# Attention and a gated MLP on one core: GpSimd makes and stores the later score bounds, weight parts go out two in ten score products, output steps pause at product ends and group changes

## The chip, the cores and the metric

The kernel runs on one core of a Trainium2 chip. The metric is the device time of one execution in microseconds (us). The engines are TensorE (PE in the profile; PEld is its loading of weights), VectorE (DVE), ScalarE (ACT), GpSimd (POOL) and SyncE (SP, which here only issues DMAs). Each engine works through its own instructions in order; waits on other engines are semaphores.

## The reference

A transformer block with pre-normalisation, 2048 rows of width 512, all in float32: attention with 32 query heads of 16 elements that share one key and one value head, then a gated MLP of width 1792.

```python
def _A_ref(x, wq, wk, wv, wo):
    B, S, D = x.shape
    H = 32
    Dh = D // H
    q = (lambda x, *d: x.transpose(*d))((x @ wq).reshape(B, S, H, Dh), 0, 2, 1, 3)
    k = x @ wk
    v = x @ wv
    scores = jnp.einsum("bhqd,bkd->bhqk", q, k) * (Dh ** -0.5)
    p = _softmax(scores, axis=-1)
    o = jnp.einsum("bhqk,bkd->bhqd", p, v)
    return (lambda x, *d: x.transpose(*d))(o, 0, 2, 1, 3).reshape(B, S, H * Dh) @ wo

def _B_ref(x, w_gate, w_up, w_down):
    return (_gelu(x @ w_gate) * (x @ w_up)) @ w_down

h = x + _A_ref(_layernorm(x, axis=-1), A_wq, A_wk, A_wv, A_wo)
h2 = h + _B_ref(_layernorm(h, axis=-1), B_w_gate, B_w_up, B_w_down)
```

## The kernel before

**Tiling.** The 2048 rows of queries are four blocks b of 512. The 32 heads are eight groups g of four. For each block and group the keys run in 16 chunks kc of 128. One score step, `score(n)`, makes two heads' scores of one key chunk (two matmuls into a tile s, 128 x 1024) and lets ScalarE take the exponential into p (L410). Two steps, n and n+1, are a pair; 32 steps are a group, 256 a block. TensorE weighs the values with p two pairs later (`weigh`, L414, accumulator acc), and after a group's last chunk `evacuate` copies acc to oT on VectorE (L427).

**Numbers in two parts.** Matmul operands are split into a high part and the rest (hi and lo), so one product is three matmuls. Queries are kept in DRAM (q_d) with a row per head for a bound on the scores, which stands in for the softmax's maximum; `load_q` (L386) brings a group's queries back as qg, two pairs after the group before it has begun.

**Block 0's stage.** Beside the scores of block 0 three things run. First, the projections of the later blocks' queries (`project_q`): a chunk's product is done in two halves of TensorE's rows, two matmuls at a time beside the scores. After the first half VectorE copies one column of the bank (mark, L210), and TensorE's second half waits for it. After the second half VectorE copies the bank out (pq_raw, L225), splits it (qh, ql), and squares it (qs). There is one bank, so the next product waits for the copy. Once a block's four chunks are done, a small matmul sums the squares per head (pqn, L259), VectorE copies it (qn, one buffer) and takes its maximum into q2, GpSimd works out two factors from it in four small instructions (`factors`, L269 to L278), and VectorE makes the bound's row m from qn and the factors (`bound`, L285), which SP stores to q_d (L289). The list `after` holds factors and bound with a count of pairs; `age` runs down the counts and places the step in the program when its count is out: factors after 2, the bound after 4.

Second, the split of the MLP's and wo's weights into parts (`part_weights`, 46 parts): SP loads 256 KB into w_raw (L514), AHEAD_W parts ahead, GpSimd casts the high part (L119) and subtracts (L120) into w_both (two buffers), and stores 512 KB to DRAM from its own queue (L523, L529). One part goes out each time the loop calls `next(parts)`: every second pair in which `after` is empty (L1109).

Third, the outputs of the groups. `evacuate` stores oT to DRAM (L431); `turn_out` (L440) reads it back with the layout turned, as oc; then VectorE inverts the sums (L454, four reciprocals), multiplies (divide, L457), and makes o_hi (L465) and o_lo (L469). In block 0 these steps wait in the list `outs`, one entry taken at the end of each pair (`take_out`), with eight empty entries between the reading back and the reciprocals.

**Order.** In this stage the order of SP, VectorE, TensorE, GpSimd and ScalarE is the order in which the program is written; nothing reorders it. At n = 256 what is left of parts and bounds is put out, and the dense work of block 0 (wo, then the MLP) begins; its tiles take the place of w_raw, w_both and the rest.

Of the kernel before, what the change touches and what calls it, by code (L numbers as in the profile page):

```python
# [9 lines left out]
F32 = mybir.dt.float32  # L10
# [9 lines left out]
P = 128  # L20
# [9 lines left out]

W2 = 3

AHEAD_W = 3

LAST_Q = 240

# [16 lines left out]
def kernel(  # L53
# [12 lines left out]
    nc = tc.nc  # L66
    x = x.flatten_outer_dims()
    out = out.flatten_outer_dims()
    S, D = x.shape
    DH = wk.shape[1]  # L70
# [9 lines left out]
    KC = S // P  # L80
# [27 lines left out]
    q_d = dram.tile([H, KR, S], F32R, name="q_d")  # L108
# [49 lines left out]
    def run(outer, first):  # L158
# [10 lines left out]
        def psum1(name):  # L169
            return ps.tile([P, T], F32, tag="d", bufs=width, name=name)  # L170
# [16 lines left out]
        def project_q(b, cs, eng, col, whole=None):  # L187
            halves = whole is not None
            whole = whole if halves else cs
            tsl = slice(b * T, (b + 1) * T)  # L190
            xT_hi, xT_lo = xT[b]
            urgent = b == 0 and cs[0] == 0
            qss = []
            for c in cs:
                pq = psum1(f"pq_{b}_{c}")
                terms = [
                    (wt[:, d, c * P : (c + 1) * P], xt[:, d, :])
                    for d in range(DC)
                    for wt, xt in ((wq_hi, xT_hi), (wq_hi, xT_lo), (wq_lo, xT_hi))
                ]  # L200
                last = len(terms) - 1
                full = c in whole
                for n, (lhsT, rhs) in enumerate(terms if full else ()):
                    nc.tensor.matmul(pq, lhsT, rhs, start=(n == 0), stop=(n == last))  # L204
                    if n % 3 == 2 and (urgent or n < last):
                        yield 3
                for a in range(2) if not full else ():
                    if a:
                        mark = eb.tile([P, 1], F32, tag="qmark", bufs=2, name=f"mark_{b}_{c}")
                        nc.vector.tensor_copy(mark, pq[:, :1])  # L210
                    rows = slice(64 * a, 64 * a + 64)
                    for n, (lhsT, rhs) in enumerate(terms):
                        yield a, last - n, partial(
                            nc.tensor.matmul, pq, lhsT[rows], rhs[rows],
                            start=(a == 0 and n == 0), stop=(a == 1 and n == last),
                            skip_group_check=True,
                        )

                raw = None
                if (b, c) in HURRY or not full:  # L220
                    raw = eb.tile([P, T], F32, tag="vT", bufs=3, name=f"pq_raw_{b}_{c}")
                    if b == 0:
                        nc.scalar.activation(raw, pq, AF.Copy)
                    else:
                        nc.vector.tensor_copy(raw, pq)  # L225
                    if full:
                        yield 3
                if halves and norms:
                    yield REST
                    norms.pop()()  # L230
                qh = eb.tile([P, T], F32R, tag="qh", bufs=2, name=f"qh_{b}_{c}")
                ql = eb.tile([P, T], F32R, tag="ql", bufs=2, name=f"ql_{b}_{c}")
                if raw is not None:
                    split(nc.vector, qh, ql, raw)
                else:

                    split(nc.vector if b == 0 and c == FIRST_Q else eng, qh, ql, pq)
                qs = eb.tile([P, T], BF16, tag="qs", bufs=DC, name=f"qs_{b}_{c}")
                square = partial(
                    (nc.gpsimd if urgent else nc.vector).tensor_tensor,  # L240
                    qs, qh.bitcast(F32), qh.bitcast(F32), op=ALU.mult,
                )
                if full:
                    square()
                else:
                    squares.append(square)
                qss.append(qs)
                for r0, part in ((0, qh), (DH, ql), (2 * DH, qh)):
                    nc.sync.dma_start(
                        q_d[c * HC : (c + 1) * HC, r0 : r0 + DH, tsl].bitcast(F32),  # L250
                        part.bitcast(F32),
                    )
                if not halves and (raw is None or b == 0):
                    yield 3

            def norm():
                pn = psum1(f"pqn_{b}_{cs[0]}")[:H, :]
                for i, c in enumerate(cs):
                    nc.tensor.matmul(  # L259
                        pn, sel[:, c, :], qss[i], start=(i == 0), stop=(i == len(cs) - 1)  # L260
                    )
                qn = eb.tile([H, T], F32, tag="qn", bufs=1, name=f"qn_{b}_{cs[0]}")
                nc.vector.tensor_copy(qn, pn)
                nc.vector.tensor_reduce(q2[:, col : col + 1], qn, axis=AX.X, op=ALU.max)

                mm = eb.tile([H, 3], F32, tag="mm", bufs=2, name=f"mm_{b}_{cs[0]}")

                def factors():
                    nc.gpsimd.tensor_scalar(  # L269
                        mm[:, 0:1], q2[:, col : col + 1], k2m, 1e-30, op0=ALU.mult, op1=ALU.add  # L270
                    )
                    nc.gpsimd.tensor_tensor(
                        mm[:, 1:2], mm[:, 0:1], power[:H, 0:1], op=ALU.pow
                    )
                    nc.gpsimd.tensor_scalar(
                        mm[:, 2:3], mm[:, 0:1], mm[:, 1:2], 0.5, op0=ALU.mult, op1=ALU.mult
                    )
                    nc.gpsimd.tensor_scalar(  # L278
                        mm[:, 1:2], mm[:, 1:2], k2m, 0.5, op0=ALU.mult, op1=ALU.mult
                    )  # L280

                m = eb.tile([H, T], F32R, tag="m", bufs=2, name=f"m_{b}_{cs[0]}")

                def bound():
                    nc.vector.tensor_scalar(  # L285
                        m, qn, mm[:, 1:2], mm[:, 2:3], op0=ALU.mult, op1=ALU.add
                    )
                    hs = slice(cs[0] * HC, (cs[-1] + 1) * HC)
                    nc.sync.dma_start(q_d[hs, 3 * DH, tsl].bitcast(F32), m[hs].bitcast(F32))  # L289

                if not urgent:
                    after.extend([[2, factors], [4, bound]])
                return qn, mm, m, factors

            if halves:
                norms.append(norm)
                return
            qn, mm, m, factors = norm()
            if urgent:
                yield 2  # L300
                factors()
                nc.scalar.activation(
                    m, qn, AF.Identity, bias=mm[:, 2:3], scale=mm[:, 1:2]
                )
                ms[b] = m
            else:
                yield 2


        after, squares, norms = [], [], []  # L310
        ms = {}
        q_first = project_q(0, range(FIRST_Q), nc.scalar, 0)
        q_rest = project_q(0, range(FIRST_Q, DC), nc.scalar, NB)
# [78 lines left out]
        o_blk, pair, outs, last_out = {}, [None], [], []  # L392
# [32 lines left out]
        def evacuate(b, g, acc):  # L425
# [61 lines left out]
            if last:  # L487
                last_out.extend([piece, gather])
            elif k == 1:

                if b == 0:
                    outs.extend([[] for _ in range(8)])
                    outs.extend([partial(invert, t)] for t in range(TB))
                    outs.extend([step] for step in (divide, high, low))
                else:
                    outs.append([])
                    outs.extend([partial(invert, t), partial(invert, t + 1)] for t in (0, 2))
                    outs.append([divide, high, low])
# [7 lines left out]
        def part_weights(pw):  # L506
# [3 lines left out]


            def load_f(src, name):
                raw = pw.tile([P, D], F32, tag="w_raw", bufs=AHEAD_W + 1, name=f"{name}r")
                nc.sync.dma_start(raw.rearrange("p (c n) -> p c n", n=src.shape[-1]), src)  # L514
                return raw

# [21 lines left out]
            for f in range(FC):  # L538
                fs = slice(f * P, (f + 1) * P)
                for k, src in enumerate((wg_t, wu_t)):  # L540
                    name = f"w1{f}_{k}"
# [4 lines left out]
                name = f"w2{f}"  # L546
# [505 lines left out]
        n, lead = 0, 2 * PER + sum(SIZES[: LEAD[0]])  # L1052
        with tc.manual_schedule(engines={mybir.EngineType.SP, mybir.EngineType.DVE}):
            parts, said = None, 3 if first else 0
            if first:
                work = later_q()
                parts = part_weights(early.enter_context(tc.tile_pool(name="parts", bufs=1)))
# [13 lines left out]
            while n < lead:  # L1071
# [6 lines left out]
                if n == 2 * PER:  # L1078
# [7 lines left out]
                    parts = work = None  # L1086
# [17 lines left out]
                    finish(1)  # L1104
                while squares:
                    squares.pop(0)()
                if outs:
                    take_out()
                if parts is not None and n % 4 == 0 and not after:  # L1109
                    next(parts, None)  # L1110
            assert n == lead
        assert not outs
# [421 lines left out]
```

## Time and profile before

| what | us |
|---|---|
| three runs, median | 1423.63 |
| three runs, lowest and highest | 1416.68, 1423.84 |
| the profiled execution | 1423.06 |
| its span, first to last instruction | 1421.1 |
| TensorE busy | 1400.7 (99%) |
| ScalarE busy | 1044.7 (74%) |
| VectorE busy | 549.0 (39%) |
| GpSimd busy | 180.1 (13%) |

The span goes from the first to the last instruction; the execution's time has what lies around it too. A share of busy time is a mean over stages. In the rows that follow, a line begins with its start in us and its length, or with its place in the code (L410); "out<-in" are the tiles that an instruction writes and reads, buffer numbers left out; in square brackets stands how long the engine was idle before and what ended that. The rows of a window give its length, then the busy time and instructions of each engine.

### The profile page before, as it was taken

How to read it: one execution, taken by the hardware profiler on the slowest of the kernel's cores; microseconds unless marked ns; L12 is line 12 of the kernel's file. 1: busy time of each engine (PE TensorE's matmuls, PEld its weight loads, DVE VectorE, ACT ScalarE, POOL GpSimd, SP SyncE). 2: the span in 40 equal slices, each digit the busy share in tenths (PEclk: the TensorE clock that was granted, in tenths of full speed). 3: DMA queues.
4: the chain of work that ended last, by engine and by line, in shares of the span. 5: the costliest groups of instructions: out<-in, count | busy, mean ns of one | idle time of the engine just before them, and what ended most of it. 6: DMA issues, size and time to landing. Idle time of an engine off the chain costs nothing.

```text
span 1421.1 us, 25578 instructions
## 1 busy us (share of the span) xinstructions
PE 1400.7 (99%) x10622; PEld 776.6 (55%) x10622; DVE 549.0 (39%) x984; ACT 1044.7 (74%) x1149; POOL 180.1 (13%) x272
## 2 busy tenths in 40 slices
PE   9999999999999999999999999999999999999998
PEld 7533333334555555555555555555565555557886
DVE  7413221314352332514252332413343342427665
ACT  7699998997787787777777777877788777772000
POOL 6365466400000000000000000000000000002000
PEclk9999999999999999999999999999999999999999
DMA  4477777733242242214252332223243241435551
GB/s 158 160 237 270 216 255 256 239 122 119 86 146 94 87 145 82 91 47 165 95 166 80 99 134 85 88 82 123 94 139 116 86 146 37 143 122 196 183 200 61
DMA packets 84699, 193.68 MB, mean 136 GB/s; under 512 B 9676, under 2 KB 24012, under 8 KB 84544
## 3 DMA queue, kind: packets, MB, share of 16 engines
q1 hardware_dynamic: 77208, 165.65, 35.4%
q0 software_dynamic: 7200, 26.22, 5.0%
q8 instruction: 85, 1.39, 0.4%
q14 instruction: 38, 0.31, 0.1%
q10 hardware_dynamic: 168, 0.10, 0.0%
HBM read 142.12 MB, written 49.55 MB: 135 GB/s over the span
## 4 chain that ended last, share of the span: by engine, by line
PE 87%; DMA 4%; ACT 3%; POOL 2%; DVE 1%; issue 1%; SPq 1%; DVEq 0%; POOLq 0%; ACTq 0%
PE acc L414 30%; PE s L406 18%; PE pu L928 9%; PE pg L928 8%; PE pd L928 5%; PE pd L605 3%; PE pd L627 3%; ACT p L410 3%; PE pg L627 3%; PE pu L627 3%; PE pp L605 2%; PE pq L404 2%; PE pq L204 1%; DMA w_0r<-in_B_w_gate_dram 1%; DMA w_d<-w_1b 1%
## 5 line engine op out<-in xcount | busy, mean ns | idle before, releaser
L410 ACT ACTIVATE p<-s 128x1024 f32<-128x1024 f32 x1024 | 973.3, 1029 | 233.9 <-PE s L406 232.0
L414 PE MATMUL acc<-p,v_sb 128*32 128x512 f32 x4096 | 499.4, 600 | 1.1 <-DVE oT L427 1.1
L406 PE MATMUL s<-qg,kaug 50*128 50x512 f32 x1984 | 419.4, 427 | 3.6 <-ACT p L410 3.6
L406 PEld LDWEIGHTS s<-qg,kaug 50*128 50x128 f32 x1984 | 191.5, 184 | 256.6 <-ACT p L410 158.3
L414 PEld LDWEIGHTS acc<-p,v_sb 128*32 128x32 f32 x4096 | 107.6, 109 | 226.7 <-issue 220.5
L928 PE MATMUL pu<-x2h,w 64*128 64x512 f32 x672 | 212.3, 391 | 0.0
L928 PE MATMUL pg<-x2h,w 64*128 64x512 f32 x672 | 211.3, 391 | 0.3 <-DVE mark_pg L951 0.2
L928 PEld LDWEIGHTS pg<-x2h,w 64*128 64x128 f32 x672 | 115.9, 185 | 15.4 <-DVE mark_pg L951 1.1
L928 PEld LDWEIGHTS pu<-x2h,w 64*128 64x128 f32 x672 | 116.1, 185 | 14.7
L928 PE MATMUL pu<-x2l,w 64*128 64x512 f32 x336 | 122.2, 391 | 0.0
L928 PE MATMUL pg<-x2l,w 64*128 64x512 f32 x336 | 122.0, 391 | 0.0
L805 ACT ACTIVATE ga<-ga 128x512 f32<-128x512 f32 x56 | 35.3, 634 | 89.2 <-DVE ga L800 89.2
L129 POOL TENSOR_SCALAR rstd<-mv 128x1 f32<-128x1 f32 x16 | 3.5, 222 | 680.4 <-DVE mv L127 680.3
L928 PE MATMUL pd<-w,gh 64*128 64x512 f32 x384 | 81.2, 392 | 0.0
L870 DVE TENSOR_TENSOR h<-h,pd 128x512 f32<-128x512 f32 x48 | 31.9, 684 | 115.4 <-PE pd L928 66.3
L1161 DVE SCALAR_TENSOR_TENSOR ga<-ga,g 128x512 f32<-128x512 f32 x70 | 48.4, 691 | 52.6 <-ACT ga L805 51.6
L454 DVE RECIPROCAL oc<-oc 128x128 f32<-128x128 f32 x64 | 56.4, 922 | 31.5 <-DMA oc<-acc_d 26.7
L789 DVE COPY g<-pg 128x512 f32<-128x512 f32 x56 | 38.7, 692 | 63.3 <-PE pg L928 57.6
L928 PEld LDWEIGHTS pu<-x2l,w 64*128 64x128 f32 x336 | 58.0, 185 | 7.1
L928 PEld LDWEIGHTS pg<-x2l,w 64*128 64x128 f32 x336 | 57.9, 185 | 7.3
L427 DVE COPY oT<-acc 128x512 f32<-128x512 f32 x32 | 22.1, 692 | 101.2 <-PE acc L414 101.0
L802 DVE SCALAR_TENSOR_TENSOR g<-g,pu 128x512 f32<-128x512 f32 x56 | 38.2, 683 | 40.2 <-PE pu L928 30.3
(244 smaller groups left out, 1430.1 us busy)
## 6 DMA issues: line engine op xcount, KB each, us to landing
w<-w_d SPq DMA_DIRECT2D x112, 512.0 KB
w<-w_d SPq DMA_DIRECT2D x28, 1024.0 KB
qg<-q_d SPq DMA_DIRECT2D x48, 200.0 KB
q_d<-qh SPq DMA_DIRECT2D x32, 256.0 KB
acc_d<-oT SPq DMA_DIRECT2D x31, 256.0 KB
oc<-acc_d SPq DMA_DIRECT2D x124, 64.0 KB
w_d<-w_0b POOLq DMA_DIRECT2D x14, 512.0 KB, 5.5
w_d<-w_1b POOLq DMA_DIRECT2D x14, 512.0 KB, 5.5
```

The source lines that it names most:

```text
L406: nc.tensor.matmul(s[:, a, :], kaug[rows, kc * P : (kc + 1) * P], qg[rows, 2 * u + a, :], start=True, stop=True,)
L410: nc.scalar.activation(p[:, 2 * u : 2 * u + 2, :], s, AF.Exp, scale=SCALE)
L414: nc.tensor.matmul(acc[32 * j : 32 * j + 32, :], v_sb[:, kc, :], p[:, j, :], start=(kc == 0), stop=(kc == KC - 1), skip_group_check=True,)
L454: nc.vector.reciprocal(oc[:, 1, sl], oc[:, 1, sl])
L605: nc.tensor.matmul(banks[k], lhsT[rows], rhs[rows], start=(turn == 0 and i == 0), stop=(turn == 1 and i == n - 1), skip_group_check=True,)
L627: nc.tensor.matmul(bank, lhsT, rhs, start=(i == 0), stop=(i == len(ts) - 1))
L789: nc.vector.tensor_copy(g, pg)
L802: nc.vector.scalar_tensor_tensor(g, g, 0.5, pu, op0=ALU.mult, op1=ALU.mult)
L805: nc.scalar.activation(a, a, AF.Tanh, scale=GELU_A * GELU_C)
L870: nc.vector.tensor_tensor(hs[t], hs[t], pd, op=ALU.add)
L928: nc.tensor.matmul(e["bank"], lhsT[rows], rhs[rows], start=i == 0 and not e["both"], stop=last and e["both"], skip_group_check=True,)
L1161: (soon or lazy).pop(0)()
```

## The change

- `bound` runs on GpSimd, right behind `factors`, two pairs after the maximum; its store to q_d goes out on GpSimd's own DMA queue. VectorE and SP lose both rows.
- A weight part goes out in two of every five pairs, whether or not a bound is due; its load stands two parts ahead in place of three. w_raw keeps its four buffers.
- No output step is taken in the two pairs after a product's copy (`pause`), nor in the pairs that end at n % 32 = 2 and 4, the second of which holds a group's evacuation. There are six empty entries in place of eight.

```diff
-AHEAD_W = 3
+AHEAD_W = 2
...
                     if full:
                         yield 3
+                    else:
+                        pause[0] = 2
...
                 def bound():
-                    nc.vector.tensor_scalar(
+                    factors()
+                    nc.gpsimd.tensor_scalar(
                         m, qn, mm[:, 1:2], mm[:, 2:3], op0=ALU.mult, op1=ALU.add
                     )
                     hs = slice(cs[0] * HC, (cs[-1] + 1) * HC)
-                    nc.sync.dma_start(q_d[hs, 3 * DH, tsl].bitcast(F32), m[hs].bitcast(F32))
+                    nc.gpsimd.dma_start(q_d[hs, 3 * DH, tsl].bitcast(F32), m[hs].bitcast(F32))
 
                 if not urgent:
-                    after.extend([[2, factors], [4, bound]])
+                    after.append([2, bound])
...
-        after, squares, norms = [], [], []
+        after, squares, norms, pause = [], [], [], [0]
...
-                    outs.extend([[] for _ in range(8)])
+                    outs.extend([[] for _ in range(6)])
...
-                raw = pw.tile([P, D], F32, tag="w_raw", bufs=AHEAD_W + 1, name=f"{name}r")
+                raw = pw.tile([P, D], F32, tag="w_raw", bufs=AHEAD_W + 2, name=f"{name}r")
...
-                if outs:
+                if outs and not pause[0] and n % (2 * KC) not in (2, 4):
                     take_out()
-                if parts is not None and n % 4 == 0 and not after:
+                pause[0] = max(pause[0] - 1, 0)
+                if parts is not None and n // 2 % 5 in (0, 2):
                     next(parts, None)
```

The rows of TensorE and of ScalarE stand as before. Three places show what moves on the others. VectorE around the product of block 3's first chunk (qn and m are those of block 2, summed up behind it), before:

```order
L427 COPY oT_4_2476<-acc_4_2123 128x512
L225 COPY pq_raw_0_2519<-pq_0_2280 128x512
L263 COPY qn_0_2545<-pqn_0_2540 32x512
L264 TENSOR_REDUCE q_70<-qn_0_2545 32x1
L119 CAST qh_0_2550<-pq_raw_0_2519 128x512
L120 TENSOR_TENSOR ql_0_2551<-pq_raw_0_2519,qh_0_2550 128x512
L1106 TENSOR_TENSOR qs_0_2554<-qh_0_2550 128x512
L285 TENSOR_SCALAR m_0_2549<-qn_0_2545,mm_0_2548 32x512
L210 COPY mark_1_2643<-pq_1_2558 128x1
```

and now:

```order
L430 COPY oT_4_2442<-acc_4_2097 128x512
L468 CAST o_hi_1865<-oc_1_1824 128x512
L225 COPY pq_raw_0_2482<-pq_0_2254 128x512
L265 COPY qn_0_2502<-pqn_0_2497 32x512
L266 TENSOR_REDUCE q_70<-qn_0_2502 32x1
L119 CAST qh_0_2507<-pq_raw_0_2482 128x512
L120 TENSOR_TENSOR ql_0_2508<-pq_raw_0_2482,qh_0_2507 128x512
L1109 TENSOR_TENSOR qs_0_2511<-qh_0_2507 128x512
L472 TENSOR_TENSOR o_lo_1866<-oc_1_1824,o_hi_1865 128x512
L210 COPY mark_1_2617<-pq_1_2515 128x1
```

The bound has gone from between qs and the mark; o_hi now stands behind oT_4 and o_lo ahead of the mark.

VectorE at the end of the third group (oT_2), before:

```order
L1106 TENSOR_TENSOR qs_1_1789<-qh_1_1785 128x512
L465 CAST o_hi_1799<-oc_0_1147 128x512
L469 TENSOR_TENSOR o_lo_1800<-oc_0_1147,o_hi_1799 128x512
L427 COPY oT_2_1840<-acc_2_1471 128x512
L210 COPY mark_2_1919<-pq_2_1793 128x1
```

and now:

```order
L1109 TENSOR_TENSOR qs_1_1780<-qh_1_1776 128x512
L430 COPY oT_2_1821<-acc_2_1457 128x512
L460 TENSOR_TENSOR oc_0_1145<-oc_0_1145 128x512
L468 CAST o_hi_1865<-oc_0_1145 128x512
L472 TENSOR_TENSOR o_lo_1866<-oc_0_1145,o_hi_1865 128x512
L210 COPY mark_2_1901<-pq_2_1784 128x1
```

The group's copy now comes ahead of the output steps.

SP's DMAs at the sixth group's end (oT_5), before:

```order
L514 DMA w212r<-in_B_w_down_dram 128x512
L431 DMA acc_d<-oT_5_2806 128x512
L440 DMA oc_2_2479<-acc_d 16x2x512 x4
L514 DMA w_0r<-in_B_w_gate_dram 128x4x128
L386 DMA qg_7_2819<-q_d 50x4x512 x2
```

and now:

```order
L517 DMA w_0r<-in_B_w_gate_dram 128x4x128
L434 DMA acc_d<-oT_5_2780 128x512
L389 DMA qg_7_2783<-q_d 50x4x512 x2
L443 DMA oc_2_2445<-acc_d 16x2x512 x4
L517 DMA w_1r<-in_B_w_up_dram 128x4x128
```

The next group's queries are loaded ahead of the outputs' reading back.

## The prediction

> **What bounds the kernel now.** I read the table of engines first, then the stage that the change touches (block 0 of the attention with the projections beside it, about 60 to 315 us) by windows, then the waits of ScalarE and TensorE there, then ScalarE's timeline, then the chain of waits at the largest gap.
>
> The page's costliest group and the waits of ScalarE and of TensorE between 60 and 330 us:
>
> ```profile
> L410 ACT ACTIVATE p<-s 128x1024 f32<-128x1024 f32 x1024 | 973.3, 1029 | 233.9 <-PE s L406 232.0
> ACT p L410 <- PE s L406: 15.4, 28, 3.7
> PE pq L404 <- DVE mark L210: 3.5, 1, 3.5
> PE acc L414 <- DVE oT L427: 1.1, 1, 1.1
> ```
>
> The exponentials are the pace of this stage. Of 15.4 us that they idle, one wait is 3.7, and TensorE shows two waits for VectorE worth a name: 3.5 us for a mark and 1.1 us for a copy of an accumulator. The next rows are windows cut at the copies of the accumulators (oT), so each is one group of four heads: length, busy times of PE, PEld, DVE, ACT and POOL, granted clock, DMA share, GB/s.
>
> ```profile
> 184.20:214.48 30.28, 30.28 (x226) 10.31 (x228) 9.26 (x13) 30.01 (x33) 17.95 (x21) 1.00 0.75 253
> 214.48:251.68 37.20, 33.68 (x230) 11.37 (x232) 7.75 (x13) 30.60 (x33) 23.17 (x30) 0.91 0.76 252
> 251.68:281.96 30.28, 30.28 (x226) 10.30 (x228) 11.33 (x15) 30.28 (x33) 15.44 (x19) 1.00 0.75 248
> ```
>
> A clean group takes 30.28 us, with ScalarE full. The one from 214.48 takes 6.92 more, and there the granted clock is 0.91. ScalarE's timeline gives the gaps one by one (start, length, what, idle before):
>
> ```profile
> 156.28 54.92 ACT L410 ACTIVATE p<-s 128x1024 f32<-128x1024 f32 x58 [1.08 <-PE s L406]
> 221.45 10.49 ACT L410 ACTIVATE p<-s 128x1024 f32<-128x1024 f32 x11 [0.70 <-PE s L406]
> 235.60 1.02 ACT L410 ACTIVATE p<-s 128x1024 f32<-128x1024 f32 x1 [3.65 <-PE s L406]
> 238.24 1.94 ACT L410 ACTIVATE p<-s 128x1024 f32<-128x1024 f32 x2 [1.62 <-PE s L406]
> 240.80 56.76 ACT L410 ACTIVATE p<-s 128x1024 f32<-128x1024 f32 x60 [0.61 <-PE s L406]
> ```
>
> And the chain of waits that leads to the large gap (start, length, what):
>
> ```profile
> 232.04 0.26 POOL mm L269
> ...
> 233.39 0.26 POOL mm L278
> 233.65 0.03 issue
> 233.68 0.53 DVE m L285
> 234.21 0.08 DVE mark L210
> 234.29 0.04 issue
> 234.33 0.79 PE pq L404
> ```
>
> GpSimd, busy with weight parts until then, reaches the factors (L269) at 232.04. VectorE's bound (L285) stands waiting for them, the mark stands behind the bound, and TensorE stands before the second half of a product, which waits for the mark. So a late helper engine stops the path through one in-order VectorE.
>
> **The change part by part.** The order listings of TensorE and ScalarE are the same in both programs row for row, so the change can only move waits.
>
> (a) The bound leaves VectorE. VectorE's rows in the stage then hold no use of a result of this GpSimd work except one: the copy qn must find its single buffer read by the bound before, which is three or four products earlier. What goes is the gap at 235: 3.65 + 1.62 + 0.61 = 5.88 us of ScalarE's idle time; by the windows it is 37.20 - 30.28 - 0.70 (the gap at 221.45, which belongs to the norm's matmul and stays) = 6.22. The 0.34 between the two are ScalarE's own starts (30.60 against 30.01 busy). The end slides with ScalarE, so I take 6.2; the bounds are 5.9 and 6.9 (nothing of the 0.70 staying).
>
> What it adds is on GpSimd: four bounds of 32x512 and four DMA issues. GpSimd has no such row; the nearest are its casts and subtractions with the same 512 elements, and its issues:
>
> ```profile
> L119 POOL CAST w_0b<-w_0r 128x512 fp32r<-128x512 f32 x14 | 8.6, 612 | 25.1 <-DMA w_d<-w_1b 17.8 <-DMA w_0r<-in_B_w_gate_dram 7.2
> L120 POOL TENSOR_TENSOR w_0b<-w_0r,w_0b 128x512 fp32r<-128x512 f32 x14 | 17.9, 1279 | 1.2
> L523 POOL DMA_DIRECT2D w_d<-w_0b x14 | 8.1, 576 | 3.9 <-POOL w_0b L120 3.9
> ```
>
> So between 0.61 and 1.28 us each (I take 0.6, one source like the cast) and 0.58 for the issue, about 5 us in all, on an engine off the path. What hides it is that the bound's row is read late. The earliest reader is group 2's load of q, issued at 93.49, 12.5 us after the store that it needs:
>
> ```profile
> 80.99 0.36 SPq L289 DMA_DIRECT2D q_d<-m  x1
> 93.49 1.32 SPq L386 DMA_DIRECT2D qg<-q_d  x2
> ```
>
> Price 0. If the cover went, SP would stand at that load with all that is queued behind it. The trace has no store of this size from GpSimd's queue; the nearest, its 1 MB loads of wo, land in 6.7 to 8.5 us (below, at c), less than 12.5, so 0 stands at both ends. The Trainium skill speaks against this edit ("SBUF — State Buffer", SBUF: two separate sides): descriptors of a DMA issued from GpSimd can't be written while VectorE holds the shared port in a fast copy, and it measured 3.1 us in place of 0.62. By that the store would be some 2.5 us later, an estimate from that page; no run here shows it yet.
>
> (b) Output steps pause. Around 150 us VectorE did this (its timeline):
>
> ```profile
> 151.79 1.51 DVE L465 CAST o_hi<-oc 128x512 fp32r<-128x512 f32 x1
> 153.33 0.69 DVE L469 TENSOR_TENSOR o_lo<-oc,o_hi 128x512 fp32r<-128x512 f32 x1
> 153.94 0.68 DVE L427 COPY oT<-acc 128x512 f32<-128x512 f32 x1
> ```
>
> The two output steps ahead of oT made TensorE wait the 1.1 us. In the new order oT_2 comes first and the division, o_hi and o_lo after it. That takes the gap of 1.08 at 156.28 away: 1.1 us. The bounds are 1.08 and, with a start of ScalarE saved, 1.2. The new place of o_hi, between oT_4 and the next copy of a product, costs at most 1.51 us where VectorE idled 2.07 (217.24, below): 0.
>
> (c) Fewer parts in a stretch, two loads ahead. A pair of score products takes 30.28 / 16 = 1.89 us. A part went out every second pair, 3.8 us; two in five pairs is 4.7. GpSimd does a part in 0.61 + 1.28 + 0.58 and the 0.28 before its issue (3.9 / 14 above), 2.75, so it has more room, and SP waits less for buffers of w_raw. None of this is on the path: 0. But the last part moves back, from 276.51 to score 242 or so, seven pairs of 1.89 us after the oT before it (281.96), less the 7.3 gained: about 288; with 2.75 for the part and 8.5 for its store it is done by 299.3. What hides it is the block behind: the load of wo waits for TensorE until 304.91 anyway and lands in 6.7 to 8.5 us, 11 us ahead of its first matmul.
>
> ```profile
> 276.51 0.62 POOL L119 CAST w213b<-w213r 128x512 fp32r<-128x512 f32 x1
> L579 POOL DMA_DIRECT2D wo<-wo_d x2: 731/760/789, 304.9 to 305.7; - x2
> DMA to landing us min/median/max: 6.7/7.6/8.5
> 324.53 0.72 PE L605 MATMUL pp<-wo,o_hi 64*128 64x512 f32 x4 [0.27 <-issue]
> ```
>
> (d) SP's order. The four loads of oc now stand behind the load of q and one pair later, with two empty steps fewer until the reciprocals. Tightest is group 5:
>
> ```profile
> 217.24 0.69 DVE L225 COPY pq_raw<-pq 128x512 f32<-128x512 f32 x1 [2.07 <-PE pq L404]
> 252.40 1.29 SPq L431 DMA_DIRECT2D acc_d<-oT  x1
> 259.68 1.74 SPq L440 DMA_DIRECT2D oc<-acc_d  x4
> 262.01 0.80 SPq L386 DMA_DIRECT2D qg<-q_d  x2
> qg<-q_d SPq DMA_DIRECT2D x48, 200.0 KB
> 263.46 0.95 DVE L454 RECIPROCAL oc<-oc 128x128 f32<-128x128 f32 x1 [5.08 <-DMA oc<-acc_d]
> 269.58 0.69 DVE L225 COPY pq_raw<-pq 128x512 f32<-128x512 f32 x1 [5.17 <-PE pq L404]
> ```
>
> VectorE waited for oc until 263.46 and was needed at 269.58. Now two reciprocals stand there: 6.12 - 2 x 0.95 = 4.2 us are left. The load of q issues in SP's wait between 253.7 and 259.7, and its 400 KB at the 252 GB/s of the window from 214.48 are 1.6 us in the same queues, so oc may be 0 to 2.4 us (with 0.80 of issue) later; it fits. I take 0.
>
> Sum: 1421.1 - 6.2 - 1.1 = 1413.8 of span; the profiled execution took 1423.06, 1.96 around its span, so **1415.8**. The median of the three runs is 0.57 above that execution. One of them took 1416.68, 7.0 below the other two: the large gap alone would be that much, but no trace shows that run, so it only says that 6.2 is a likely size.
>
> **The rivals.**
>
> Late oc (the slower side): the reciprocals of groups 1, 3 and 5 stand ahead of a mark or a product's copy; if oc lands more than 4.2 us later than now, VectorE blocks again just as at 234. For it: SP's wait for acc_d reached 6 us here, and the loads follow 400 KB more. Against it: 2.4 us is all that I can find, and fewer weights move meanwhile. A stop of 3.5 us costs 6.2 as measured, clock included, at each place: 1422.0 with one, 1428.2 with two, 1434.4 with all three. Slower than before from two places on. The Trainium skill ("TensorE: Matmul & The Clock Gate", Part 1) puts the loss of clock at an idle window of about 3.4 us. By that a stop of 1 to 2 us costs itself alone, and the rival at three places of 2 us would end at 1421.8; the window with the 3.65 us gap, at a clock of 0.91 where its neighbours have 1.00, fits it.
>
> Late parts: GpSimd was 10.8 us behind its data at 232. The maximum of q that its factors read was there at 221.25:
>
> ```profile
> 220.58 0.67 DVE L264 TENSOR_REDUCE q<-qn 32x1 f32<-32x512 f32 x1
> ```
>
> If it is as late at the end of the stage, or later, the dense block's loads wait for buffers of the parts. wo's first matmul is then at 324.53 - 7.3 = 317.2, its load must go out 8.5 us ahead, and the parts are done at 299.3: beyond 9.4 us of lateness each us is one on the path. At 10.8 us that gives 1417.2, at 16 us 1422.4. Against it: the slower pace leaves GpSimd 40% of its time.
>
> Half of it: the chain from a product's end to its mark gets longer elsewhere. The cast at 151.79 took 1.51 where the copy after it, of as many elements, took 0.68: VectorE's times vary, and GpSimd now has four bounds more beside it. If waits of 1 us came at four of the ten marks, (a) would keep 2.2 of 6.2: 1419.8. Against it: no mark but the one at 234 shows a wait now.
>
> That the change doesn't do what it says: VectorE's row for qn does wait for GpSimd. It would need GpSimd to be three products late, and I leave it at nothing.
>
> **How the numbers follow.** The forecast has 0.61, with a range of its own of 1413.5 to 1418; late oc 0.15 (0.08 of it at all three places), late parts 0.12, half of it 0.12. A difference of 0.5%, 7.1 us, is about what a measurement of this kernel can tell from no change, so faster by that begins at 1416.5, which the forecast passes by 0.7 us only. Of its 0.61 I put 0.48 below that line and 0.13 above, and 0.04 of late parts and of half of it, in their mildest forms, below: faster 0.52. Slower begins at 1430.7 and needs late oc at all three places: 0.08. The rest, 0.40, is within 0.5%. The range of 8 in 10 is 1413.0 to 1423.5: it leaves out late oc at two and three places, some 0.11, and the ends of the others, some 0.08.
>
> **What would show it.** In the new profile: the window of the sixth group at about 30.9 in place of 37.20 with the clock at 1.00; no ScalarE gap over 1 us between 117 and 310; TensorE's waits without the mark (3.5) and without oT (1.1); oT before o_hi at the third group's end; the bound on GpSimd at 0.6 to 1.3 us; the last part near 288; the reciprocals without a wait that ends behind a mark's product. The prediction is wrong if TensorE waits for a mark or a copy again, whatever VectorE then stood at, or if the dense block's first matmul (324.53) comes less than 6 us earlier.

## The result, and the profile after

| kernel | runs | median us | lowest to highest | runs under 1420 |
|---|---|---|---|---|
| before | 22 | 1421.25 | 1416.68 to 1424.82 | 8 |
| changed | 22 | 1417.76 | 1416.24 to 1424.18 | 21 |

The ratio of changed to before is 0.9978, with a 95% interval of 0.9969 to 0.9987: 0.2% faster, so within 0.5%. The lowest times of the two lie 0.4 us apart. The change hardly lowers what the kernel can reach; it makes most executions reach it. The profiled execution of the changed kernel took 1416.82, its span 1415.1, against 1423.06 and 1421.1 before.

TensorE's and ScalarE's waits between 60 and 330 us in the profile after (engine, line, what it waited for: us in total, times, longest):

```profile
ACT p L413 <- PE s L409: 11.5, 25, 2.8
PE s L409 <- ACT p L413: 1.7, 4, 0.7
PE pp L608 <- DMA qg<-q_d: 0.4, 1, 0.4
```

The waits for the mark (3.5) and for oT (1.1) are gone. The longest wait of ScalarE, 2.8, was there before, at the start of the dense block. The windows from oT to oT, cut as those of before (length, busy time of PE, PEld, DVE, ACT and POOL, granted clock, DMA share, GB/s):

```profile
183.06:213.34 30.28, 30.28 (x226) 10.31 (x228) 7.64 (x11) 30.00 (x33) 16.69 (x20) 1.00 0.79 251
213.34:244.51 31.17, 31.17 (x230) 10.76 (x232) 10.11 (x15) 30.41 (x33) 22.34 (x29) 1.00 0.74 246
244.51:274.78 30.27, 30.27 (x226) 10.29 (x228) 8.83 (x12) 30.27 (x33) 12.26 (x15) 1.00 0.82 239
```

The sixth group takes 31.17 us where it took 37.20, and the clock stays at 1.00. ScalarE's timeline (start, length, what, idle before) has one unbroken stretch of 81 us, over the place of the gap for oT, and one of 70 where the large gap was:

```profile
128.63 81.42 ACT L413 ACTIVATE p<-s 128x1024 f32<-128x1024 f32 x86 [0.85 <-PE s L409]
210.33 9.27 ACT L413 ACTIVATE p<-s 128x1024 f32<-128x1024 f32 x10 [0.28 <-ACT p L413]
220.36 70.02 ACT L413 ACTIVATE p<-s 128x1024 f32<-128x1024 f32 x74 [0.76 <-PE s L409]
```

GpSimd at the sixth group's factors and bound, from its timeline:

```profile
217.71 1.27 POOL L120 TENSOR_TENSOR w28b<-w28r,w28b 128x512 fp32r<-128x512 f32 x1
220.29 0.36 POOL L271 TENSOR_SCALAR mm<-q,k2m 32x1 f32<-32x1 f32 x1 [1.31 <-DVE q L266]
...
223.03 0.75 POOL L288 TENSOR_SCALAR m<-qn,mm 32x512 fp32r<-32x512 f32 x1
```

GpSimd reaches the factors 1.31 us before their data and stands waiting for VectorE. Before, it reached them at 232.04, some 11 us after the data. The bound has moved onto GpSimd, but GpSimd also comes 11.75 us sooner, and that is not the bound's doing: with the bound alone moved it comes at 231.54 (e1, below). So two edits, not one, could claim the gap.

VectorE's timeline in the seventh group shows the price of the new order on SP:

```profile
260.46 1.76 DVE L457 RECIPROCAL oc<-oc 128x128 f32<-128x128 f32 x2 [9.25 <-DMA oc<-acc_d]
262.41 0.69 DVE L225 COPY pq_raw<-pq 128x512 f32<-128x512 f32 x1 [0.18 <-PE pq L407]
```

The reciprocals end their wait for oc 0.18 us ahead of the product's copy: the slack is used up almost to the end.

### The profile page after: what moved, and what is told of

It is laid out like the page before. It is cut to its first block, busy times and chain, and to the rows that moved or that the text cites. A ratio compares the mean times of both kernels' runs of the same rounds, so it can differ in the third digit from the quotient of the medians.

```text
span 1415.1 us, 25570 instructions
## 1 busy us (share of the span) xinstructions
PE 1396.9 (99%) x10622; PEld 776.2 (55%) x10622; DVE 549.1 (39%) x980; ACT 1044.2 (74%) x1149; POOL 187.0 (13%) x280
## 4 chain that ended last, share of the span: by engine, by line
PE 92%; ACT 3%; DMA 2%; DVE 1%; issue 1%; POOL 0%; SPq 0%; DVEq 0%; ACTq 0%; POOLq 0%
PE acc L417 33%; PE s L409 20%; PE pu L931 10%; PE pg L931 7%; PE pd L931 4%; PE pd L608 3%; PE pd L630 3%; PE pg L630 3%; PE pu L630 3%; ACT p L413 2%; PE pq L407 2%; PE pp L608 2%; PE pq L204 1%; PE pp L739 1%; PE pxt L675 1%
```

## The experiments

Two theories were held from the first results on. P, the prediction's: the waits for mark and oT are the loss, the moved bound and the pauses remove them, and the pace is worth nothing. Q: the pace of the weight parts is the cause, since it decides how late GpSimd and SP come to everything else. R and S came later. The table holds all runs; "factors" is when GpSimd starts the sixth group's factors (their data is there at about 220.3 where nothing has stopped before), and the last column is what TensorE waited for DVE and DMA between 60 and 310 us, both in the profiled execution.

| kernel | median us (lowest, highest) | ratio, 95% interval | factors | TensorE's waits over 1 us |
|---|---|---|---|---|
| e1 bound alone | 1422.71 (1417.95, 1425.23) | 1.0010, 0.9994 to 1.0026 | 231.54 | oT 1.2 |
| e2 all but the bound | 1417.03 (1415.78, 1421.37) | 0.9980, 0.9969 to 0.9992 | 220.26 | none |
| e3 pauses alone | 1424.48 (1421.89, 1426.28) | 1.0022, 1.0011 to 1.0032 | 234.46 | mark 7.1 |
| e4 eight empty entries | 1417.72 (1415.94, 1419.74) | 0.9980, 0.9970 to 0.9990 | 220.77 | none |
| c1 pace alone | 1417.87 (1416.19, 1421.02) | 0.9977, 0.9963 to 0.9990 | 221.89 | oT 1.5 |
| c2 all but the pace | 1418.18 (1417.11, 1422.98) | 0.9979, 0.9965 to 0.9992 | 238.19 | qg 3.8 in two |
| c3 pace and bound | 1419.10 (1416.21, 1423.66) | 0.9988, 0.9973 to 1.0003 | 224.30 | oT 1.9 |
| e6 three empty entries | 1426.71 (1422.02, 1428.47) | 1.0034, 1.0018 to 1.0049 | 227.13 | pq_raw 6.0 in two |
| c6 bound, nine empty | 1423.39 (1417.41, 1427.83) | 1.0009, 0.9992 to 1.0026 | 234.85 | oT 2.0, qg 1.5 |
| c7 order, bound on VectorE | 1417.91 (1415.64, 1421.57) | 0.9978, 0.9966 to 0.9990 | 222.18 | none |
| c8 bound alone again | 1425.0 (one run) | | 233.83 | pq_raw 4.5 |
| c9 pauses alone again | 1424.09 (one run) | | 233.40 | mark 6.0 |

Ratios are to the kernel before on the same chip; each of the first ten had 12 runs. c3's 224.30 and e6's 227.13 follow TensorE's earlier stops (c3's oT of the fifth group is 3.7 us later than in the changed kernel; e6's GpSimd was waiting for its data), so they are not lateness.

**e1, the bound alone.** The kernel before with the bound and its store on GpSimd:

```diff
                 def bound():
-                    nc.vector.tensor_scalar(
+                    factors()
+                    nc.gpsimd.tensor_scalar(
...
-                    nc.sync.dma_start(q_d[hs, 3 * DH, tsl].bitcast(F32), m[hs].bitcast(F32))
+                    nc.gpsimd.dma_start(q_d[hs, 3 * DH, tsl].bitcast(F32), m[hs].bitcast(F32))
...
-                    after.extend([[2, factors], [4, bound]])
+                    after.append([2, bound])
```

> Before, with the bound alone moved to GpSimd (and its store to GpSimd's queue); pace of the parts, loads and output steps as before. If VectorE's standing behind late factors is the loss (first theory): TensorE waits for no mark over 1 us however late GpSimd is, the 1.1 us wait for oT stays, the time is 2 to 6 us below before's. If the slower pace of the parts brings the gain (rival): the time is within 1 us of before's, and a gap near 235 us stays.

It gained nothing (1.001), although its profile has no wait for a mark. Neither theory had it whole: the mark's wait went, as the first said, but the gain did not come; the rival's gap near 235 is not there either, and the median lies 1.75 us above that of the kernel before on the same chip, which the interval does not tell from none. Three of its views, SP's timeline, GpSimd's and VectorE's, show why:

```profile
245.19 0.35 SPq L515 DMA_DIRECT2D w212r<-in_B_w_down_dram  x1
248.06 0.37 SPq L515 DMA_DIRECT2D w_0r<-in_B_w_gate_dram  x1
248.48 0.61 SPq L249 DMA_DIRECT2D q_d<-qh  x1
...
253.04 1.45 SPq L432 DMA_DIRECT2D acc_d<-oT  x1
260.32 1.73 SPq L441 DMA_DIRECT2D oc<-acc_d  x4
```

```profile
243.56 1.61 POOL L120 TENSOR_TENSOR w_1b<-w_1r,w_1b 128x512 fp32r<-128x512 f32 x1
```

```profile
241.83 0.43 DVE L119 CAST qh<-pq_raw 128x512 fp32r<-128x512 f32 x1
245.91 0.69 DVE L428 COPY oT<-acc 128x512 f32<-128x512 f32 x1 [1.90 <-PE acc L415]
...
264.01 0.95 DVE L455 RECIPROCAL oc<-oc 128x128 f32<-128x128 f32 x1 [11.40 <-DMA oc<-acc_d]
264.88 0.63 DVE L225 COPY pq_raw<-pq 128x512 f32<-128x512 f32 x1
```

qh was ready at 242.26 and its store went out at 248.48; oT was ready at 246.60 and its store went out at 253.04, 6.4 us late. SP stood at two loads of weight parts: a part's raw tile comes free only when GpSimd has subtracted, and GpSimd's subtraction ended at 245.17. So oc came late, and VectorE waited 11.40 us for it with the product's copy behind: TensorE lost 0.4 us here. This was the prediction's "late oc", through SP's queue.

**c8, the same kernel profiled again**, to catch one of its slower executions.

> A second look at the bound alone on GpSimd, eight of whose twelve runs took 1421 to 1425 us where the profiled one took 1418.5. Theory R: if this execution is one of the slow ones, VectorE's reciprocal ends its wait for oc after the product's end, TensorE waits 2 to 5 us for pq_raw or mark near 265, and the granted clock falls there to about 0.9. Theory S: no such wait, and the time is lost elsewhere.

It was one: 1425.0, span 1423.3 against 1416.8. Its waits of TensorE, its windows 217 to 255 and 255 to 286, and VectorE's timeline:

```profile
PE pq L405 <- DVE pq_raw L225: 4.5, 1, 4.5
```

```profile
217.00:255.00 38.00, 38.00 (x280) 13.38 (x276) 7.09 (x12) 37.10 (x41) 25.51 (x34) 1.00 0.77 257
255.00:286.00 31.00, 26.51 (x178) 8.52 (x176) 8.59 (x13) 23.71 (x26) 12.43 (x15) 0.89 0.61 215
```

```profile
267.16 0.95 DVE L455 RECIPROCAL oc<-oc 128x128 f32<-128x128 f32 x1 [15.54 <-DMA oc<-acc_d]
268.03 0.63 DVE L225 COPY pq_raw<-pq 128x512 f32<-128x512 f32 x1
```

The sixth group is clean and the loss has moved one group on: oc 3.15 us later than in e1's profile (though the stage ran 1.0 us earlier), TensorE's wait longer by 4.1, the clock at 0.89, the span longer by 6.5. That is the gap of before, at another instruction. Theory R (the wait for oc takes the place of the wait for the factors) holds for this kernel.

**c6, the bound alone with nine empty entries.** One more entry puts the reciprocal behind the product's copy.

```diff
-                    outs.extend([[] for _ in range(8)])
+                    outs.extend([[] for _ in range(9)])
```

> The bound alone on GpSimd (pace, loads and outputs' steps as before) with nine empty entries where that kernel had eight: by VectorE's order the one reciprocal that stood ahead of the second product's copy of pq in the sixth group now stands behind it, at GpSimd, SP and TensorE next to nothing moves. Theory R (the bound alone gained nothing because the wait for oc, 11.4 us long in its profile, took the place of the wait for m): 1417 to 1419 us, ratio 0.997 to 0.999, no copy of pq behind a wait for oc; the oT wait of 1.2 us may go or stay. Theory S (its loss lies elsewhere, in GpSimd's store or its port, or in the dense block's start): as the bound alone, 1421.5 to 1424 us.

The wait for oc at the copy went, as R said, but the time did not (1423.39), as S said. Its timeline of TensorE holds two other stops:

```profile
155.60 1.07 PE L415 MATMUL acc<-p,v_sb 128*32 128x512 f32 x8 [1.99 <-DVE oT L428]
...
157.73 1.94 PE L415 MATMUL acc<-p,v_sb 128*32 128x512 f32 x8
...
276.50 0.70 PE L407 MATMUL s<-qg,kaug 50*128 50x512 f32 x1 [1.51 <-DMA qg<-q_d]
277.98 1.93 PE L415 MATMUL acc<-p,v_sb 128*32 128x512 f32 x8
```

The copy oT stood behind output steps for 1.99 us, and the next group's queries (qg) came 1.51 us late. R was right on the mechanism and wrong to take it for the only one: behind the wait for oc stood a wait for qg, which SP issues after the same late stores (266.83 here, 246.83 in the changed kernel).

**e3, the pauses alone, and c9, the same profiled again.** The kernel before with the pauses and the group rule, eight empty entries:

```diff
                     if full:
                         yield 3
+                    else:
+                        pause[0] = 2
...
-        after, squares, norms = [], [], []
+        after, squares, norms, pause = [], [], [], [0]
...
-                if outs:
+                if outs and not pause[0] and n % (2 * KC) not in (2, 4):
                     take_out()
+                pause[0] = max(pause[0] - 1, 0)
```

> Before, with the pauses of the output steps alone (eight empty entries, bound on VectorE, parts every second pair). If o_hi and o_lo ahead of oT cost the 1.1 us: no TensorE wait for oT, no ScalarE gap of 1.08 near 156 us, the time 1.1 us below before's, with before's gap near 235 us still there. If not: the 1.1 us appears at another group, and the time is before's.

> A second look at the kernel before with the pauses alone (the same kernel as in the run of that name; 1421.9 to 1426.3 us): the wait of TensorE for mark near 235 was 7.1 us, behind factors that GpSimd ended late. If that wait is what spreads its time from run to run: another length of it here, 3 to 9 us, and a time that is shorter or longer by about as much as the wait and the slower clock behind it (6 to 7 us lost for 3.5 us waited in the profile of the kernel before).

Slower than before (1.0022), where 1.1 us less was expected, and no run was under 1420. The wait for oT is gone and the wait for the mark is longer: ScalarE's timeline of e3, then of c9:

```profile
238.01 1.02 ACT L412 ACTIVATE p<-s 128x1024 f32<-128x1024 f32 x1 [7.23 <-PE s L408]
```

```profile
236.96 1.02 ACT L412 ACTIVATE p<-s 128x1024 f32<-128x1024 f32 x1 [6.16 <-PE s L408]
```

The stage runs some 1.1 us earlier and GpSimd does not (its factors start at 234.46 and 233.40, before at 232.04; why later was not found), so the bound is late by more. Of one kernel, 1.1 us less of this wait went with a span 1.2 us shorter (1423.4 and 1422.2): the length of this one stop differs from execution to execution, and the time with it.

**c1, the pace alone.** The kernel before with

```diff
-AHEAD_W = 3
+AHEAD_W = 2
...
-                raw = pw.tile([P, D], F32, tag="w_raw", bufs=AHEAD_W + 1, name=f"{name}r")
+                raw = pw.tile([P, D], F32, tag="w_raw", bufs=AHEAD_W + 2, name=f"{name}r")
...
-                if parts is not None and n % 4 == 0 and not after:
+                if parts is not None and n // 2 % 5 in (0, 2):
```

> The kernel before with the weight parts' new pace, two loads ahead and their two more buffers, nothing else: the bound stays on VectorE at 4 with the factors at 2, eight empty entries, no pauses. Theory P (the prediction's: the gain is the bound's move, the pace is worth nothing): as before, ratio 0.999 to 1.001, a wait of TensorE for mark as long as before's (3.5 us in its profile). Theory Q (since the kernel without the moved bound was as fast as the changed one: the pace keeps GpSimd free when a group's factors come due, so VectorE's bound is never late): 1416.5 to 1418.5 us, ratio 0.997 to 0.9985, no wait of TensorE for mark, VectorE's wait for mm of the factors at most 7 us at a time; the oT wait of 1.1 us at the third group's end stays.

1417.87, as fast as the whole change: Q. One sign of Q missed: VectorE's longest wait for the factors was 9.05 us, not 7, at 301.44, where TensorE did not wait for it. The bound is still on VectorE and still behind the factors. VectorE's row of the sixth group's bound in the kernel before:

```profile
233.68 0.53 DVE L285 TENSOR_SCALAR m<-qn,mm 32x512 fp32r<-32x512 f32 x1 [10.38 <-POOL mm L278]
```

In c1, the timelines of GpSimd, VectorE and SP:

```profile
221.89 0.33 POOL L269 TENSOR_SCALAR mm<-q,k2m 32x1 f32<-32x1 f32 x1
```

```profile
223.99 0.53 DVE L285 TENSOR_SCALAR m<-qn,mm 32x512 fp32r<-32x512 f32 x1 [0.57 <-POOL mm L278]
229.93 0.16 DVE L210 COPY mark<-pq 128x1 f32<-128x1 f32 x1 [5.41 <-PE pq L404]
242.03 0.99 DVE L119 CAST qh<-pq_raw 128x512 fp32r<-128x512 f32 x1
246.10 0.69 DVE L427 COPY oT<-acc 128x512 f32<-128x512 f32 x1 [1.76 <-PE acc L414]
```

```profile
243.05 0.60 SPq L249 DMA_DIRECT2D q_d<-qh  x1
...
247.90 2.26 SPq L431 DMA_DIRECT2D acc_d<-oT  x1
255.20 1.75 SPq L440 DMA_DIRECT2D oc<-acc_d  x4
```

VectorE waits 0.57 us for the factors in place of 10.38, and stands ready 5.41 us before the mark. qh is ready at 243.02 and stored at 243.05; oT is ready at 246.79 and stored 1.1 us later, where e1 needed 6.4. The pace takes both delays away at their source. GpSimd ends the last part ahead of the factors just as their data comes (221.79 and 221.75), and SP asks for a raw tile that was freed a part earlier (of part i - 2, not i - 1). By GpSimd's rows 36 parts stand ahead of these factors in the kernel before and 31 in c1 and in the changed kernel. Five fewer, at 2.75 us of work each, are some 14 us (an estimate from the rows); GpSimd came 10 to 12 us sooner. It was not only at work in the kernel before: between 203.8 and 232.0 it stood 8.8 us, in four waits, for its own stores of earlier parts to land and free w_both. Which of the two halves of the edit, the slower pace or the earlier free tile, does more was not tried, nor was a third buffer for w_both.

**e2, all but the bound, and c7, the same with eight empty entries.** The changed kernel with the bound back on VectorE and SP:

```diff
-                    after.append([2, bound])
+                    after.extend([[2, factors], [4, bound]])
```

> The changed kernel with the bound back on VectorE and its store on SP (factors after 2 pairs, bound after 4). First theory: VectorE still stands behind GpSimd wherever that is late; the time lies 2 to 6 us above the changed kernel's. Rival (pace): with parts in two of five pairs GpSimd reaches the factors before q's maximum is there, as in the changed kernel's trace at 220.29, VectorE waits under 2.5 us for the bound and TensorE for no mark; the time is within 1 us of the changed kernel's.

> The changed kernel with the bound back on VectorE and SP (factors at 2, bound at 4) and eight empty entries: pace, loads and pauses of the change, and three of four reciprocals of the sixth group behind the copy of pq. If the three waits (m, oc, oT) are all that the change can gain here: 1416 to 1417.5 us, level with the changed kernel without the moved bound (1417.03), lowest near 1415.5, and no run above 1420. If the bound on GpSimd were worth something of its own: 1 us or more slower than the changed kernel, 1418.5 to 1420 us.

1417.03 and 1417.91, level with the changed kernel: moving the bound adds nothing once the pace is there. In e2 VectorE waited 0.51 us for the sixth group's factors; its longest wait for factors, 6.7 us at 80, cost TensorE nothing. c7 lies 0.4 above its forecast, and its two runs above 1421 missed its "no run above 1420".

**c2, all but the pace, and c3, pace and bound.** c2 is e1 with the pauses of e3; c3 is c1 with the bound of e1.

> The changed kernel with the kernel before's pace (a part in every fourth step when nothing is pending, three loads ahead) and eight empty entries: the bound on GpSimd and the pauses stay. Theory P: as the changed kernel, 1416.5 to 1418.5 us, since both waits that it names (mark 3.5, oT 1.1) are answered by these two edits. Theory Q: no faster than the kernel before, 1420.5 to 1424.5 us, ratio 0.9995 to 1.0025, because GpSimd's casts still stand ahead of the factors and so of the bound's store, and the waits move to the loads of qg or to VectorE's reciprocals.

> The kernel before with the new pace and the bound on GpSimd, without the pauses, eight empty entries. Theory P: the bound's 6 us of the changed kernel's gain and the oT wait of 1.1 us left, 1417.5 to 1419 us. Theory Q: as the pace alone, 1417 to 1419 us, with the oT wait of 1.1 us. The two differ here only in whether this is faster than the pace alone (P: by 3 us; Q: not).

c2 is P's answer, 1418.18 where Q said 1420.5 or more. Together the bound and the pauses do what neither does alone: the pauses put the reciprocals behind the product's copy, so e1's wait for oc has no copy behind it. Its GpSimd is as late as ever (238.19), its profiled execution (1422.98, the slowest of the 12) stood 3.8 us for qg, and nine of its 12 runs were under 1420. So the pace is enough but not the only way. c3, 1419.10, lies 0.1 above both ranges and is no faster than the pace alone, as Q said; its wait of 1.86 us for oT is the one that the pauses remove.

**e4 and e6, the empty entries.** The changed kernel with eight or three in place of six:

```diff
-                    outs.extend([[] for _ in range(6)])
+                    outs.extend([[] for _ in range(3)])
```

> The changed kernel with eight empty entries in place of six: the sixth group's reciprocals then stand behind the product's copy. If late oc is what lifts some of the changed kernel's executions (up to 1424): VectorE's row for pq_raw near 262 us shows 5 us of idle time in place of 0.18, the spread of the runs shrinks and the median falls by 0 to 1.5 us. If oc is not involved: median and spread as the changed kernel's, within 0.5 us.

> The changed kernel with three empty entries where it has six, so that the reciprocals of the first outputs stand about six steps earlier in VectorE's order. In the changed kernel's profile the last of them ended its wait for oc 0.18 us before VectorE's copy of pq. If oc's lateness is a wait in the making (the prediction's rival of a late oc): VectorE waits for oc ahead of that copy, TensorE waits for pq_raw or mark 3 to 10 us near 235 to 265, 1420 to 1430 us. If oc is in time by more than the trace shows: within 0.1% of the changed kernel, 1416.5 to 1419 us.

Eight is the same as six (1417.72), though the reciprocals now stand behind the copy: late oc does not set the changed kernel's median. Three costs 8 to 9 us against the changed kernel: TensorE waits twice for pq_raw, of which the first, in VectorE's timeline, is

```profile
197.24 0.95 DVE L457 RECIPROCAL oc<-oc 128x128 f32<-128x128 f32 x1 [13.47 <-DMA oc<-acc_d]
198.11 0.63 DVE L225 COPY pq_raw<-pq 128x512 f32<-128x512 f32 x1
```

So late oc is a real wall, and the change stands 0.18 us ahead of it in its profile. No kernel tried beats the changed one by more than the runs can tell.

## Why the prediction was right in its number and wrong in its reasons

**The time.** 1417.76 lies 2.0 us above the forecast of 1415.8, inside the range. The sum of 7.3 came out in place: the third group's oT moved from 153.94 to 152.79 (1.15, forecast 1.1), the sixth group's from 251.68 to 244.51 (7.17), and the dense block's first matmul from 324.53 to 317.46 (7.07). By the end of the span 6.0 is left; 1.1 us is given back over the 1100 us that follow, at no one place. Every sign that the prediction named came true or nearly so: the sixth group's window is 31.17 us at a clock of 1.00, both waits are gone, the bound takes 0.75 us, the last part starts at 291.31. None of these signs could tell the moved bound from the pace. That the number came out is in part luck: the edit that was priced at 0 was in the same change as the one that was credited.

**What the sum was made against.** The large gap of before is not one size (e3 and c9 show two lengths of it in one kernel). The execution with the profile lay 1.8 us above the median of 22 runs, and 8 of these 22 were under 1420, too fast for a stop of that size, though no trace shows one of them. A term read from one execution was taken as the kernel's. Over medians the gain is 3.5 us, not 7.3.

**(a), credited with 6.2, was the wrong step to credit.** "The bound leaves VectorE" alone gains nothing (e1), and without it the change is as fast (e2). The wait at the mark does go, but one group later VectorE stands at oc instead (c8: 4.5 us, clock 0.89, span +6.5). The prediction had that rival at 0.15 and looked for its cause in the change's own order on SP. The cause was older: SP stood behind GpSimd's parts, which the gap at the mark had hidden.

**(c), priced at 0, was the step that failed.** The prediction saw of GpSimd that "it has more room, and SP waits less for buffers of w_raw" and went on "None of this is on the path: 0". GpSimd was on the path in the very chain quoted: the factors came late because parts stood ahead of them, and because GpSimd, called busy there, also stood for its own stores. The pace alone gives 0.9977. With the factors on time, the bound on VectorE costs no wait (0.57 where it was 10.38). The dense block did not wait for the last part (forecast near 288).

**(b)** was right in place (1.1) and wrong as a term of its own: alone it makes the kernel slower (e3), because what comes sooner waits longer for GpSimd. Nor is its wait always there: c8 is the same kernel as e1, with the same two steps ahead of oT, and its TensorE did not wait, because VectorE's rows were shorter (ql 0.69 us where e1 has 1.66, o_lo 0.69 where e1 has 1.65).

**(d)** was mis-sized. oc was put at 0 to 2.4 us later against a slack of 4.2; it ended its wait 0.18 us ahead of need, so 4.0 of the 4.2 are gone. In the changed kernel's SP timeline the load of qg now stands ahead:

```profile
245.23 1.51 SPq L434 DMA_DIRECT2D acc_d<-oT  x1
246.83 3.09 SPq L389 DMA_DIRECT2D qg<-q_d  x2
251.90 1.71 SPq L443 DMA_DIRECT2D oc<-acc_d  x4
```

From the start of oc's issue to the reciprocal are 8.56 us (251.90 to 260.46) where before there were 3.78 (259.68 to 263.46). The issue itself comes 7.4 us after the copy oT, before 8.0, so all of the lateness lies between issue and landing. In the sixth group's profiles it goes with SP's order: 3.7 to 5.8 us where oc goes out ahead of qg (before, e1, c8, c1, c3), 8.6 where it goes out behind (the changed kernel, e2). That it is the queries' 400 KB in the same queues is argued, not shown.

**The parts do not add.** Alone the bound gives nothing, the pauses lose 0.2%, the pace gains 0.2%; bound and pauses together gain 0.2%, and all three no more. All of them shift one slack between the same three late things: the factors, oc and qg.

**The store from GpSimd's queue.** The changed kernel's four rows of it:

```profile
L292 POOL DMA_DIRECT2D q_d<-m x4: 579/581/612, 81.5 to 296.1; - x4
DMA to landing us min/median/max: 2.0/5.1/6.0
```

An issue took 0.58 to 0.61 us, as the ones for weights. The 3.1 us that the prediction quotes from the Trainium skill ("SBUF — State Buffer", SBUF: two separate sides) are for a DMA from that queue beside a fast copy of VectorE. This case does not test that: by its rows VectorE was idle at each of the four issues (between 222.45 and 228.33 for the one at 224.07).

**Open.** One of the 22 runs of the changed kernel took 1424.18. It has no trace; with 0.18 us of slack a stop at oc would explain it, and e4, with its reciprocals behind that copy, had none in 12 runs, which is too few to say.

## What to carry to other kernels

When an in-order engine shows a wait, ask what made its releaser late before moving the waiter: a helper that works off a backlog delays everything behind it, and taking one victim out of the line only shows the next. Try each part of a change alone, since parts that feed on one slack do not add. And before pricing a stop from one profile, look at the spread of the runs: a kernel whose times spread by 8 us may have a stop that is not always there.

## What the runs showed of the hardware

At one place of this kernel a stop of TensorE costs about itself up to 1.53 us, and twice itself at 1.86. This stop for oT at the third group's end was 1.21 us in e1, 1.53 in c1, 1.86 in c3 and 1.99 in c6. TensorE's timelines of c1 and of c3 around it:

```profile
155.18 1.07 PE L414 MATMUL acc<-p,v_sb 128*32 128x512 f32 x8 [1.53 <-DVE oT L427]
157.06 1.06 PE L414 MATMUL acc<-p,v_sb 128*32 128x512 f32 x8
```

```profile
155.72 1.07 PE L415 MATMUL acc<-p,v_sb 128*32 128x512 f32 x8 [1.86 <-DVE oT L428]
157.86 1.94 PE L415 MATMUL acc<-p,v_sb 128*32 128x512 f32 x8
161.05 1.06 PE L415 MATMUL acc<-p,v_sb 128*32 128x512 f32 x8
```

After the longer stop eight matmuls take 1.94 us in place of 1.06, from about 157 to 160.6. The windows from 156 to 186, of c1 and then of c3, have clocks of 1.00 and 0.94:

```profile
156.00:186.00 30.00, 30.00 (x228) 10.30 (x224) 3.42 (x7) 29.23 (x31) 12.26 (x15) 1.00 0.78 232
```

```profile
156.00:186.00 30.00, 30.00 (x214) 10.06 (x210) 3.82 (x6) 27.24 (x29) 12.32 (x15) 0.94 0.75 210
```

The fifth group's oT is then 3.73 us later than in the changed kernel (217.07 and 213.34), in c1 1.64 (214.98): twice the stop, not once. The Trainium skill ("TensorE: Matmul & The Clock Gate", Part 1) puts the loss of clock at an idle window of about 3.4 us; here less than 1.9 us was enough, and in c6 a stop of 1.51 us for qg was followed by eight matmuls of 1.93 as well, while one of 1.80 us for o_hi in c1 (at 323.72) was followed by a clock of 1.00, so the length of the stop alone does not set it. The slow stretch of some 3.5 us fits the same section's time to warm up again.
